# A spectral layer and an MLP on one core: the prologue's loads, splits and fillers rearranged, and the MLP's matmuls issued in a fixed order

## The chip, the core and the metric

The kernel runs on one core of one Trainium2 chip. The core has a matrix engine (TensorE, "PE" in the profile, with its weight loads as "PEld"), three engines for elementwise work (VectorE "DVE", ScalarE "ACT", GpSimd "POOL"), SyncE ("SP"), which here only issues DMAs, and 16 DMA engines shared by all queues. Every engine runs its own instructions in order and waits for others through semaphores. The metric is the device time of one execution in microseconds; lower is better. Three executions of the kernel before took 2612.57, 2615.16 and 2617.0 us, median 2615.16.

## The reference

```python
X = np.fft.rfft(x, axis=1)                      # x: (8, 3008, 256), float32
Yr = Xr @ w_r - Xi @ w_i + b_r                  # w_r, w_i: 256 x 256
Yi = Xr @ w_i + Xi @ w_r + b_i
Yr = np.sign(Yr) * np.maximum(np.abs(Yr) - 0.01, 0.0)   # and the same for Yi
y = np.fft.irfft(Yr + 1j * Yi, n=3008, axis=1)
h = y.reshape(24064, 256) @ w_in                # w_in: 256 x 2048, float64
out = np.maximum(0.01 * h, h) @ w_out           # w_out: 2048 x 256, float64
```

Per batch of 3008 positions: a real Fourier transform along the sequence, a complex 256 x 256 projection with a bias and a soft threshold, the inverse transform; then, over all 24064 tokens, an MLP with a leaky rectifier.

## The kernel before

The transform of 3008 = 47 x 64 points is done in two factors, so it becomes small matrix products. A batch passes three stages. `fwd(b)` is the first: it loads x in seven chunks (six of 512 columns, one of 256), folds the two halves, multiplies by `fa` and writes the result u to DRAM. For batch 1 alone the fold is left out, and `stage_a1(c)` makes chunk c with plain float32 products: eight TensorE matmuls for a wide chunk, two ScalarE copies from PSUM, two SyncE writes. `mid(b)` is the second: 12 steps that load u (`load(j)`, two steps ahead), do the second factor (`stage_b`), the projection, bias and threshold (`proj`), and the inverse's first factor (`stage_g`), whose result v is copied by ScalarE and written to DRAM by two DMAs. `inverse(pi, eh)` is the third: it loads v as `vin`, multiplies by `ga` into a PSUM bank of the tag psf, and with VectorE and ScalarE writes tokens into the tile `yc`.

The MLP (`moe`) works on 47 chunks of 512 tokens. `forms(ci)` makes seven combinations of the four quarters of a chunk (one level of Strassen's scheme) and splits each into a high and a low float32r part, the tiles `yh` and `yl`. A chunk has eight steps q. In a step `moe_a` does four of the seven products and `moe_b` three, each as three float32r matmuls of 256 columns (high by high, low by high, high by low): 12 and 9 matmuls into two PSUM banks of the tag psh. Between them ScalarE copies a product (p), VectorE adds to make u and two more sums in place; `moe_b`'s products accumulate in the same banks, so they wait for these sums. Then VectorE adds (gf), ScalarE applies the rectifier, casts to the high part gh, and VectorE subtracts to make the low part gl. `moe_o(ci, q, eh)` multiplies gh and gl by w_out: six matmuls of 512 columns for each of two halves of the output, two steps (LAG) after the step that made them. The last of a chunk is copied and written to `out`.

What sets the order: the program is written as one sequence, and a planner places each instruction on its engine, by program order and by its own estimate of when inputs and buffers are free. So an engine's queue may hold instructions in another order than the program's. `tc.issue_after(ins)` orders what is issued inside it behind `ins`, on the engine of `ins` only; it is an order in a queue, not a wait on a result. Tiles of one tag share its buffers, and a new tile waits until the oldest holder has been read.

The prologue runs batch 0's `fwd` and `mid` with nothing of the MLP beside them. In it, w_in (stored as float64) is loaded in four parts and converted to float32 pairs (`convert_win`), batch 1's x is loaded, and w_out is loaded by `load_wout`: two reads of 512 KB ordered behind `reads[13]` (a u load) into the buffers of the tag gl, six more into the buffers e and z as these come free. Each of the eight parts of w_out is then converted by three ScalarE and seven VectorE instructions (`float64_parts` and lines 192 to 194); part 0 is converted anywhere in the prologue, the others behind the first chunk's last split (`made`). Five chunks of `stage_a1` follow batch 0's `mid`, behind its last-but-one product (`turning[NPAIR - 2]`); chunks 4 and 5 come at the third and fifth half step of the MLP in program order. `split_consts` splits the projection's weights, `gb` and `fa` into float32r pairs for the other batches, at the ninth half step, behind `made`. Its source `w32` holds a buffer of the tag yl, in which `forms` also places its yl and `stage_a1` its chunk 4. After the first chunk, the other batches' `fwd` and `mid` are spread between the MLP's half steps by a fraction of the work done.

Of the kernel before, what the change touches and what calls it, by code (L numbers as in the profile page):

```python
# [20 lines left out]
P = 128  # L21
# [9 lines left out]
def spectral_mlp_kernel(  # L31
# [48 lines left out]

    def block(dst, l, r, start=False):

        for i, (a, b) in enumerate(((l[0], r[0]), (l[0], r[1]), (l[1], r[0]))):
            nc.tensor.matmul(dst, a, b, start=start and i == 0, stop=i == 2, skip_group_check=True)  # L84
# [47 lines left out]
    made, converted = [], []  # L132
# [34 lines left out]
    def load_wout():  # L167
# [5 lines left out]
        def load(early):  # L173
# [3 lines left out]
            with tc.issue_after(reads[13 if early else -1].ins):  # L177
                sync.dma_start(raw.rearrange("p (a f) w -> p a (f w)", a=n), ov[:, k * n:(k + 1) * n, :])
# [24 lines left out]
    reads, written, turned, turning, thresholded = [], [], [], [], []  # L203
# [6 lines left out]
    def fwd(b):  # L210
# [107 lines left out]
    def mid(b):  # L318
# [4 lines left out]
        pool.memset(zero, 0.0)  # L323
# [94 lines left out]
        def stage_g(j):  # L418
# [6 lines left out]
            for c in range(2):  # L425
                act.dma_start(vd[c, 2 * j:2 * j + 2, :N2, :].rearrange("k n d -> n k d"), v[c * N2:(c + 1) * N2])
# [30 lines left out]
    y_t, v_t, f_t, h_t, g_t, o_t = {}, {}, {}, {}, {}, {}  # L457
# [16 lines left out]
    def inverse(pi, eh):  # L474
# [8 lines left out]
        for c in range(2):  # L483
            for i in range(2):
                o = c * ne + i * n0 * NK1
                nc.tensor.matmul(py[:, o:o + P], vin[:, c, i, s], consts["ga"][:, c, :], start=True, stop=True)  # L486
# [7 lines left out]
        while lo < p0[pi + 1]:  # L494
# [4 lines left out]
            act.copy(f_t[ci][:, eh, lo - ci * NT:hi - ci * NT], y[:, lo - p0[pi]:hi - p0[pi]])  # L499
            lo = hi  # L500

    def forms(ci):
# [7 lines left out]
        def split(k, w):  # L510
            cp = act.copy(yh[:, k], w)  # L511
            return dve.tensor_sub(yl[:, k], w, yh[:, k].bitcast(F32)), cp  # L512
# [12 lines left out]
        if ci == 0:  # L525
            made[:] = last
# [28 lines left out]
    def moe_b(ci, q):  # L555
# [11 lines left out]
        act.copy(gh, g)  # L567
        gl = sb.tile([P, 4, HT], F32R, name="gl", tag="gl")
        dve.tensor_sub(gl, g, gh.bitcast(F32))  # L569
        g_t[ci, q] = (gh, gl)  # L570

    def moe_o(ci, q, eh):
# [6 lines left out]
        for i in range(2):  # L579
            f = 2 * q + i  # L580
            for j, (a, r) in enumerate(((wh, gh), (wl, gh), (wh, gl))):
                nc.tensor.matmul(  # L582
                    po, a[:, f, s], r[:, i], start=(f == 0 and j == 0), stop=(f == NF - 1 and j == 2),
                )
# [28 lines left out]
    def moe():  # L613

        for i, (ci, q) in enumerate(steps):
            if q == 0:
                nxt = tokens(ci + 1) if ci + 1 < nch else iter(())
            moe_a(ci, q)
            if i >= LAG:
                moe_o(*steps[i - LAG], 0)  # L620
            next(nxt, None)
            yield ci + (q + 0.5) / NQ
            if i >= LAG:
                moe_o(*steps[i - LAG], 1)
            moe_b(ci, q)
# [228 lines left out]
```

## Time and profile before

| what | value |
|---|---|
| median of three executions | 2615.16 us |
| the profiled execution | 2613.38 us |
| its span, first to last instruction | 2611.6 us |
| first matmul of the MLP (L84) | 122.1 us |
| last conversion of w_out ends | about 202 us |
| last matmul of `stage_b` (batch 7) starts | 2218.9 us |
| DMA traffic | 165.14 MB, 62 GB/s of HBM over the span |

The profile is of one execution. An engine's row gives busy time, share of the span and the count of instructions. A group's row gives the line of the kernel, engine, operation, the tile written and the tiles read, shapes, the count, then busy time and the mean of one in ns, then the engine's idle time just before them and what ended it. A row of the timeline gives start, length, instruction, and in brackets the idle time ahead of it. SPq and ACTq are DMA issues on SyncE's and ScalarE's queues. A stretch's row is explained where it is shown. Matmuls overlap, so the length of one is more than the distance between two starts.

### The profile page before, as it was taken

What the parts mean: (1) busy time and instruction counts of PE and PEld (TensorE: products, weight loads), DVE (VectorE), ACT (ScalarE), POOL (GpSimd) and SP (SyncE); (2) the same over time, 40 slices, a digit from 0 to 9 for tenths busy, and PEclk for the clock granted to TensorE, in tenths of its full rate; (3) what the DMA queues carried; (4) which work ended last, traced back from release to release, by engine and by line L of the source; (5) the groups of instructions that cost most, each with busy time, mean ns of one, the idle gap of its engine ahead of it and who ended that gap; (6) DMA issues with size and microseconds to landing.
All of it is one profiled execution on the core that took longest, in us unless ns stands there. A gap on an engine that the chain in (4) does not pass through costs nothing. (4 is left out here: it accounts for less than half of the span.)

```text
span 2611.6 us, 42622 instructions
## 1 busy us (share of the span) xinstructions
PE 2555.1 (98%) x16300; PEld 2284.0 (87%) x16300; DVE 1855.0 (71%) x3403; ACT 1655.3 (63%) x3174; POOL 236.7 (9%) x180
## 2 busy tenths in 40 slices
PE   6899999999999999999999999999999999999998
PEld 4578898899889998999989999899998899988887
DVE  5687777776767778677777777777777677665664
ACT  4766675676656666567656666566665666655554
POOL 0000112000210002000121001200012000000000
PEclk8999999999999999999999999999999999999999
DMA  9622113211221113211132211321113211100000
GB/s 267 169 64 59 47 45 109 65 48 51 82 74 52 45 48 86 73 53 54 34 100 63 61 44 37 107 72 48 37 39 112 62 49 41 43 25 24 17 9 17
DMA packets 118437, 165.14 MB, mean 63 GB/s; under 512 B 13437, under 2 KB 69401, under 8 KB 118233
## 3 DMA queue, kind: packets, MB, share of 16 engines
q1 hardware_dynamic: 78193, 116.07, 14.6%
q10 hardware_dynamic: 40040, 46.34, 7.0%
q8 instruction: 128, 2.10, 0.3%
q14 instruction: 76, 0.62, 0.1%
HBM read 86.60 MB, written 75.76 MB: 62 GB/s over the span
## 5 line engine op out<-in xcount | busy, mean ns | idle before, releaser
L84 PE MATMUL psh<-yh,win_hi 128*128 128x256 f32 x2632 | 737.5, 284 | 8.5 <-DVE u L549 4.8
L84 PE MATMUL psh<-yl,win_hi 128*128 128x256 f32 x2632 | 735.3, 281 | 0.8 <-DVE yl L512 0.8
L84 PE MATMUL psh<-yh,win_lo 128*128 128x256 f32 x2632 | 724.8, 280 | 0.0
L582 PE MATMUL pso<-gh,wout_hi 128*128 128x512 f32 x1504 | 598.1, 398 | 7.1 <-ACT gh L567 6.6
L569 DVE TENSOR_TENSOR gl<-gf,gh 128x1024 fp32r<-128x1024 f32 x376 | 466.0, 1240 | 194.0 <-ACT gh L567 192.2
L582 PE MATMUL pso<-gh,wout_lo 128*128 128x512 f32 x1504 | 591.9, 394 | 0.1
L582 PE MATMUL pso<-gl,wout_hi 128*128 128x512 f32 x1504 | 557.3, 396 | 2.7 <-DVE gl L569 1.4
L84 PEld LDWEIGHTS psh<-yh,win_hi 128*128 128x128 f32 x2632 | 493.7, 189 | 34.1 <-DVE u L549 6.2
L84 PEld LDWEIGHTS psh<-yl,win_hi 128*128 128x128 f32 x2632 | 497.6, 189 | 23.7 <-DVE yl L512 1.9
L84 PEld LDWEIGHTS psh<-yh,win_lo 128*128 128x128 f32 x2632 | 493.1, 189 | 3.0
L565 ACT ACTIVATE gf<-gf 128x768 f32<-128x768 f32 x376 | 315.5, 846 | 239.8 <-DVE gf L563 229.8
L563 DVE TENSOR_TENSOR gf<-psh,u 128x512 f32<-128x512 f32 x376 | 258.3, 687 | 236.9 <-PE psh L84 235.2
L567 ACT CAST gh<-gf 128x1024 fp32r<-128x1024 f32 x376 | 394.5, 1050 | 15.6 <-ACT gf L565 9.6
L582 PEld LDWEIGHTS pso<-gl,wout_hi 128*128 128x128 f32 x1504 | 282.7, 188 | 67.7 <-DVE gl L569 12.6
L582 PEld LDWEIGHTS pso<-gh,wout_hi 128*128 128x128 f32 x1504 | 282.9, 188 | 52.4 <-ACT gh L567 11.2
L582 PEld LDWEIGHTS pso<-gh,wout_lo 128*128 128x128 f32 x1504 | 283.1, 188 | 48.9 <-DVE wout_lo L194 0.7
L562 ACT ACTIVATE gf<-psh 128x256 f32<-128x256 f32 x376 | 144.8, 385 | 194.6 <-PE psh L84 174.6
L385 POOL TENSOR_TENSOR kb<-bias,kc 128x512 f32<-128x512 f32 x84 | 118.5, 1410 | 1543.9 <-ACT kc L382 1272.9
L548 ACT COPY p<-psh 128x256 f32<-128x256 f32 x376 | 139.3, 370 | 97.5 <-PE psh L84 91.5
L549 DVE TENSOR_TENSOR u<-psh,p 128x256 f32<-128x256 f32 x376 | 157.2, 418 | 47.8 <-ACT p L548 45.7
L551 DVE TENSOR_TENSOR gf<-psh,u 128x256 f32<-128x256 f32 x376 | 155.8, 418 | 21.0 <-PE psh L84 11.8
L552 DVE TENSOR_TENSOR gf<-psh,gf 128x256 f32<-128x256 f32 x376 | 156.4, 420 | 6.3
(134 smaller groups left out, 3260.8 us busy)
## 6 DMA issues: line engine op xcount, KB each, us to landing
u<-u_dram SPq DMA_DIRECT2D x192, 128.0 KB, 2.7
v_dram<-v ACTq DMA_DIRECT2D x192, 128.0 KB, 2.4
out_dram<-ob SPq DMA_DIRECT2D x94, 256.0 KB, 2.0
vin<-v_dram SPq DMA_DIRECT2D x96, 240.0 KB, 3.3
xin<-x_dram SPq DMA_DIRECT2D x85, 240.0 KB, 2.9
u_dram<-xin ACTq DMA_DIRECT2D x72, 240.0 KB, 2.4
win_raw<-w_in_dram SPq DMA_DIRECT2D x8, 512.0 KB, 6.7
raw<-w_out_dram SPq DMA_DIRECT2D x8, 512.0 KB, 6.5
```

The costliest lines, as they stand in the source:

```text
L84: nc.tensor.matmul(dst, a, b, start=start and i == 0, stop=i == 2, skip_group_check=True)
L385: pool.tensor_add(kb, bias, kc.unsqueeze(1).broadcast_to([P, 2, D]))
L548: act.copy(p1, b1[:, lo])
L549: dve.tensor_add(u2, b1[:, hi], p1)
L551: dve.tensor_add(g[:, 3], b2[:, hi], u2)
L552: dve.tensor_add(g[:, 3], b2[:, lo], g[:, 3])
L562: act.activation(g[:, 0], b1[:, lo], AF.Prelu, alpha=SLOPE)
L563: dve.tensor_add(g[:, 1:3], b2.rearrange("p (k n) -> p k n", k=2), u2.unsqueeze(1).broadcast_to([P, 2, HT]))
L565: act.activation(g[:, 1:4], g[:, 1:4], AF.Prelu, alpha=SLOPE)
L567: act.copy(gh, g)
L569: dve.tensor_sub(gl, g, gh.bitcast(F32))
L582: nc.tensor.matmul(po, a[:, f, s], r[:, i], start=(f == 0 and j == 0), stop=(f == NF - 1 and j == 2),)
```

## The change

Seven edits go together. (1) `split_consts` runs right after batch 0's first stage instead of in the MLP. (2) The v of batch 0 is written to DRAM by SyncE instead of ScalarE. (3) w_out is read by DMAs that GpSimd issues, ordered only behind the first memset of GpSimd in `mid(0)`; the first conversion is ordered behind `made` like the others. (4) Batch 1's first stage is spread: chunks 0 and 1 inside the last steps of `mid(0)`, chunks 2 and 3 behind the last product of `stage_g`, the small chunk 6 behind the first chunk's last inverse, chunks 4 and 5 behind a gh cast and a gl subtraction of the MLP. Their order behind `turning[NPAIR - 2]` goes. (5) Chunks 0 to 3 use the PSUM tag psh, the others psf. (6) Every part of the MLP (a, half of o, b) is ordered on TensorE behind the last matmul of the part before. (7) The program order in a step becomes a, first half of o, b, second half of o; it was a, both halves, b.

```diff
+    mlp = []
+    def in_order(part, *args):
+        with tc.issue_after(mlp[0].ins) if mlp else nullcontext():
+            part(*args)
...
-            nc.tensor.matmul(dst, a, b, start=start and i == 0, stop=i == 2, skip_group_check=True)
+            mlp[:] = [nc.tensor.matmul(dst, a, b, start=start and i == 0, stop=i == 2, skip_group_check=True)]
...
-            with tc.issue_after(reads[13 if early else -1].ins):
-                sync.dma_start(raw.rearrange("p (a f) w -> p a (f w)", a=n), ov[:, k * n:(k + 1) * n, :])
+            with tc.issue_after(zeroed[0].ins):
+                pool.dma_start(raw.rearrange("p (a f) w -> p a (f w)", a=n), ov[:, k * n:(k + 1) * n, :])
...
-            pas = [(bank("psf", 2) if c in (4, 5) else bank("psh", 4))[:PA, :n] for _ in range(2)]
+            pas = [(bank("psh", 4) if c < 4 else bank("psf", 2))[:PA, :n] for _ in range(2)]
             for h in range(2):
-                with tc.issue_after(turning[NPAIR - 2].ins):
-                    products(pas[h], [
-                        (consts[f"fa{h}32"], (x_t[c][0],)), (consts[f"fa{2 * h}32"], (x_t[c][1],))])
+                products(pas[h], [
+                    (consts[f"fa{h}32"], (x_t[c][0],)), (consts[f"fa{2 * h}32"], (x_t[c][1],))])
...
-        pool.memset(zero, 0.0)
+        cleared = pool.memset(zero, 0.0)
+        if b == 0:
+            zeroed.append(cleared)
...
-                act.dma_start(vd[c, 2 * j:2 * j + 2, :N2, :].rearrange("k n d -> n k d"), v[c * N2:(c + 1) * N2])
+                (act if b else sync).dma_start(
+                    vd[c, 2 * j:2 * j + 2, :N2, :].rearrange("k n d -> n k d"), v[c * N2:(c + 1) * N2])
...
+        inverted[:] = [cp, mm]
...
+        cp = act.copy(gh, g)
...
+        parted[:] = [cp, dve.tensor_sub(gl, g, gh.bitcast(F32))]
...
-                nc.tensor.matmul(
+                mlp[:] = [nc.tensor.matmul(
                     po, a[:, f, s], r[:, i], start=(f == 0 and j == 0), stop=(f == NF - 1 and j == 2),
-                )
+                )]
...
-            moe_a(ci, q)
+            in_order(moe_a, ci, q)
             if i >= LAG:
-                moe_o(*steps[i - LAG], 0)
+                in_order(moe_o, *steps[i - LAG], 0)
             next(nxt, None)
             yield ci + (q + 0.5) / NQ
+            in_order(moe_b, ci, q)
             if i >= LAG:
-                moe_o(*steps[i - LAG], 1)
-            moe_b(ci, q)
+                in_order(moe_o, *steps[i - LAG], 1)
...
         act.mul(fa32[:, 2], fa32[:, 1], -1.0)
+        split_consts()
...
         if i == 13:
             next(wout)
+        if i >= 14:
+            if i < 16:
+                next(fp.gen)
...
-    fp.to(0.69)
+    for _ in range(2):
+        with tc.issue_after(turning[-1].ins):
+            next(fp.gen)
...
+    with tc.issue_after(inverted[-1].ins), tc.issue_after(inverted[-2].ins):
+        next(fp.gen)
     for _ in forms(0):
         pass
-    next(wout)
+    with tc.issue_after(made[0].ins):
+        next(wout)
...
         if i in (2, 4):
-            with tc.issue_after(made[0].ins):
+            with tc.issue_after(parted[0].ins), tc.issue_after(parted[1].ins):
                 next(fp.gen)
-        if i == 8:
-            with tc.issue_after(made[0].ins), tc.issue_after(made[1].ins):
-                split_consts()
```

More of the change, by code (lines that the diff above doesn't have):

```diff
@@ L201, in spectral_mlp_kernel @@
     v_dram = {}
-    reads, written, turned, turning, thresholded = [], [], [], [], []
+    reads, written, turned, turning, thresholded, zeroed = [], [], [], [], [], []
     NX = -(-NS // 2)
@@ L485, in inverse @@
                 o = c * ne + i * n0 * NK1
[L486 removed]
+                mm = nc.tensor.matmul(py[:, o:o + P], vin[:, c, i, s], consts["ga"][:, c, :], start=True, stop=True)
         odd = sb.tile([P, 2 * NG * NK1], F32, name="odd", tag="odd", bufs=1)[:, :ne]
@@ L525, in forms @@
         if ci == 0:
-            made[:] = last
+            made[:] = [last]
         yield
```

14 lines of the change are left out of this document (6 added, 8 removed).

## The prediction

> **What bounds the kernel now.** I read the page first, then the table of stretches, then the groups and the timeline of the stretches that lose time.
>
> ```profile
> span 2611.6 us, 42622 instructions
> PE 2555.1 (98%) x16300; PEld 2284.0 (87%) x16300; DVE 1855.0 (71%) x3403; ACT 1655.3 (63%) x3174; POOL 236.7 (9%) x180
> ```
> ```profile
> 139.00:201.40 62.40, 55.14 (x317) 47.53 (x316) 57.70 (x118) 39.89 (x72) 0.00 (x0) 0.92 0.18 53
> 201.40:2281.80 2080.40, 2072.35 (x13593) 1885.80 (x13593) 1521.06 (x2786) 1363.24 (x2641) 235.88 (x174) 1.00 0.21 61
> 2281.80:2597.80 316.00, 311.52 (x1931) 272.81 (x1929) 189.88 (x352) 164.32 (x295) 0.00 (x0) 1.00 0.05 17
> 2597.80:2611.60 13.80, 7.57 (x27) 5.64 (x25) 3.33 (x4) 4.63 (x6) 0.00 (x0) 0.85 0.10 38
> ```
>
> Columns: stretch, length, then busy time (count) of TensorE, its weight loads, VectorE, ScalarE, GpSimd, the granted clock, DMA share, GB/s. TensorE is the bound. No edit changes the number of matmuls, so only its lost time can go. From 201.4 to 2281.8 it idles 2080.4 - 2072.35 = 8 us; the loss sits in the prologue and the tail.
>
> The busy share hides some of it, since overlapping matmuls count as busy. So I take the spacings from the tail's timeline and the counts from its groups.
>
> ```profile
> 2506.60 0.28 PE L84 MATMUL psh<-yh,win_hi 128*128 128x256 f32 x1
> 2510.37 0.28 PE L84 MATMUL psh<-yh,win_lo 128*128 128x256 f32 x1
> ...
> 2515.98 0.40 PE L582 MATMUL pso<-gl,wout_hi 128*128 128x512 f32 x1
> 2517.83 0.28 PE L84 MATMUL psh<-yh,win_hi 128*128 128x256 f32 x1
> ```
> ```profile
> L84 PE MATMUL psh<-yh,win_hi 128*128 128x256 f32 x393 | 110.4, 283 | 0.1
> L582 PE MATMUL pso<-gh,wout_hi 128*128 128x512 f32 x224 | 90.4, 403 | 3.3 <-ACT gh L567 3.3
> ```
>
> The 33 matmuls of 256 columns start within 3.77 us, 0.118 each; eight of 512 within 1.85 us, 0.231 each. A step of the MLP has 21 and 12: 5.25 us. The tail (2281.8 to 2597.8, no spectral work left) holds three such groups of 393 and three of 224; 80 of its 1931 matmuls remain, the inverse's, which have 128 columns and which I set at 0.1 (an estimate, below the 0.118 of 256): 139 + 155 + 8 = 302 us in 316. **The tail loses 14 us**, 0.24 a step, mostly waiting for gh.
>
> The start of the MLP, 139 to 201.4, holds some ten steps:
>
> ```profile
> L84 PE MATMUL psh<-yh,win_hi 128*128 128x256 f32 x74 | 24.1, 326 | 6.4 <-DVE u L549 2.8 <-ACT gf L562 1.6 <-DVE gf L563 1.4
> L194 DVE TENSOR_TENSOR wout_lo<-cva,cvq 128x512 fp32r<-128x512 f32 x7 | 4.8, 681 | 0.0
> L128 DVE TENSOR_SCALAR raw<-cva 128x512 uint32<-128x512 uint32 x7 | 3.0, 422 | 0.1
> ```
>
> Of its 317 matmuls 3x74 at 0.118 and the rest at no more than 0.231 make 26 + 22 = 48 us, less some 2 for short ones, in 62.4: **16 us lost**, while VectorE is busy for 57.7 of 62.4. VectorE bounds this stretch: seven conversions of w_out run in it, each four instructions like L194 and three like L128, 4.0 us.
>
> **The change part by part.**
>
> *Splits early, and the second batch's chunks 4 and 5 after a gh and gl exist.*
>
> ```profile
> 134.16 1.03 DVE L512 TENSOR_TENSOR yl<-yc,yh 128x256 fp32r<-128x256 f32 x2 [6.43 <-ACT xin L286]
> 137.75 0.69 DVE L105 TENSOR_TENSOR wr_lo<-w,wr_hi 128x512 fp32r<-128x512 f32 x1
> 140.10 0.47 DVE L105 TENSOR_TENSOR fa_lo<-fa,fa_hi 120x120 fp32r<-120x120 f32 x2
> ...
> 125.50 8.87 PE L78 MATMUL psf<-xin,fa 120*120 120x512 f32 x16 [1.00 <-DVE y L492]
> 142.18 0.39 PE L84 MATMUL psh<-yh,win_hi 128*128 128x256 f32 x1 [2.77 <-DVE u L549]
> ```
>
> The first chunk's yl needs a buffer of its tag; one holds w32 until the splits are done, the other the second batch's chunk 4. So VectorE idles 6.43 us, and then u stands behind the splits while TensorE waits 2.77 us. Early splits free w32's buffer, and 6.43 us of VectorE's bound stretch start sooner. Against that stands the first conversion of w_out, now tied behind made: +4.0 us, less the splits (L105: three at 0.69, three at 0.28): 2.9 us. Net 6.4 + 2.9 - 4.0 = 5.3 us. Chunks 4 and 5 move 8.87 us of matmuls into a stretch with 16 us free. I take **-5**; ends +2 (conversions stay the limit) and -9 (all of 6.4 and 2.8).
>
> Where the splits go is idle:
>
> ```profile
> 30.88 0.69 DVE L114 TENSOR_TENSOR w<-w_i,w 128x512 f32<-128x512 f32 x1 [7.36 <-DMA w_i<-w_i_dram]
> 32.69 3.75 PE L349 MATMUL psh<-fb,u 128*128 128x128 f32 x16 [11.44 <-DMA u<-u_dram]
> ```
>
> Both engines wait there on loads. Six ScalarE casts and six subtractions of at most 0.69 fit beside the first stage B. I cost them at 0; if the weights landed later, ScalarE's first ef copy would come up to 2.6 us late.
>
> *Spread first stage.* Two chunks go ahead of the end of batch 0's middle.
>
> ```profile
> 90.71 1.13 PE L78 MATMUL psh<-zf,w 128*128 128x512 f32 x2 [1.20 <-ACT zf L406]
> 97.00 1.13 PE L78 MATMUL psh<-zf,w 128*128 128x512 f32 x2 [1.36 <-ACT zf L406]
> 100.75 2.04 PE L78 MATMUL psh<-zf,w 128*128 128x512 f32 x2 [2.63 <-ACT zf L402]
> 113.56 5.31 PE L78 MATMUL psh<-xin,fa 120*120 120x512 f32 x12
> ```
>
> Gaps of 5.2 us take 16 matmuls at 5.31/12 = 0.44, 7.1 us. Their four ScalarE copies wait only where ScalarE waits on the same chain. But this work filled the time from 102.6 until the inverse (first matmul at 111.0):
>
> ```profile
> L486 PE MATMUL psf<-ga,vin x832: 270/275/348, 111.0 to 2486.9; 120*128 120x128 f32 x167
> 123.37 1.13 PE L486 MATMUL psf<-ga,vin 120*128 120x128 f32 x8 [0.87 <-DVE y L492]
> ```
>
> There chunks 2 and 3 (7.1 us) are left for 8.4 us, and the four inverses, which alternate with ScalarE and VectorE, run with nothing beside them until the small chunk: I estimate 4 us of idle against the 2 us of before (0.87, 1.00). Net 5.2 - 1.3 - 2: **-2**; ends -5 and +3.
>
> *Results by SyncE, w_out by GpSimd.*
>
> ```profile
> L426 ACTq DMA_DIRECT2D v_dram<-v x192: 581/600/1750, 54.0 to 2241.8; - x192
> 99.24 0.59 ACT L424 COPY v<-psh 128x512 f32<-128x512 f32 x1 [1.41 <-issue]
> ...
> 20.00:32.00 12.00, 1.25 (x5) 0.55 (x3) 1.80 (x3) 2.81 (x7) 0.00 (x0) 0.65 0.93 290
> 157.08 27.68 SPq L178 DMA_DIRECT2D raw<-w_out_dram x4
> ```
>
> 24 issues of 0.6 us leave ScalarE's queue, but most lie under a running instruction; the visible one cost 1.41. On SyncE each waits for ScalarE's v, and the u loads behind it wait too; these are issued two steps ahead of their use, which covers a v that is late by less than a step. I take -1 (0 to -4, and +1 if that cover fails once). The w_out reads lose their place behind reads[13]: they follow only GpSimd's first memset and the gl buffers, free once the second group of u has been written, about 21 us. Two reads of 512 KB then share DMAs at 290 GB/s that carry batch 0's u to DRAM and back, for which TensorE waits 11.44 us. Wholly ahead they cost 1.05 MB/290 = 3.6 us, wholly behind 0. I take +2, as the queue is 0.93 full. The later reads no longer hold SyncE for 27.68 us; nobody there needs it before the next u loads, so 0. A GpSimd DMA has no row; beside the landing of SyncE's I allow the reads 0 to 2 us more each, with buffers for two conversions.
>
> **Prologue: -5 - 2 - 1 + 2 = -6 us.**
>
> *MLP in fixed order.* Each step becomes a (12 matmuls, 1.42 us), half of o (6 at 0.231: 1.39), b (9, 1.06), other half.
>
> ```profile
> L567 ACT CAST gh<-gf 128x1024 fp32r<-128x1024 f32 x56 | 58.4, 1042 | 0.2
> L565 ACT ACTIVATE gf<-gf 128x768 f32<-128x768 f32 x56 | 44.9, 839 | 58.2 <-DVE gf L563 58.2
> L563 DVE TENSOR_TENSOR gf<-psh,u 128x512 f32<-128x512 f32 x56 | 38.7, 691 | 90.5 <-PE psh L84 90.2
> ...
> 2508.82 0.41 DVE L549 TENSOR_TENSOR u<-psh,p 128x256 f32<-128x256 f32 x1
> 2510.78 1.23 DVE L569 TENSOR_TENSOR gl<-gf,gh 128x1024 fp32r<-128x1024 f32 x1 [1.54 <-ACT gh L567]
> ```
>
> After b come gf 0.69, activation 0.84, gh 1.04, gl 1.23: 3.8 us. Between b and the o that reads them lie o, a, o, b, o, a: 8.1 us. So no o can wait, and the 3.3 us on gh go. b needs p, u and two more sums of u's size after a: p (a quarter of gh's elements, at most 0.4) starts while a's last six matmuls run, so 0.4 + 3x0.41 - 0.7 = 0.9 us, under 1.39. The last step gains too:
>
> ```profile
> 2600.68 0.76 PE L582 MATMUL pso<-gh,wout_hi 128*128 128x512 f32 x1 [2.63 <-ACT gh L567]
> ```
>
> With 18 o matmuls behind the last b (4.2 us) gh comes in time, and the slow clock of that stretch (0.85) goes: -4 (0 to -4.5). Of the tail's 14 I take -10 (0 to -14), of the middle's 8 idle us -4 (0 to -8), since there the inverse and the spectral work still interrupt. **MLP: -18.**
>
> Sum -24. The profiled execution took 2613.38 us, 1.8 beside its span, and lies 1.8 under the median 2615.16: 2591.
>
> **The rivals.**
>
> 1. *Slower: b waits for VectorE.* The fixed order takes 1.39 us from the slack ahead of b, and behind a waiting b all of TensorE's queue stands: the other half of o, the next a, the spectral matmuls. If gl of step i is served ahead of u of step i+1, the sums are ready 3.8 + 3x0.41 = 5.05 us after b; o, a, o last only 4.20: 0.85 us a step. Before it was 5.59. It decides where VectorE picks gl first. Price: 0.85 in each of 56 tail steps, 48. The middle has 2080/310 = 6.7 us a step, some 0.7 of other matmuls in that path, so 0.15 x 310 = 46. With the prologue's -6, without the -18: 2703 everywhere; on half of the steps 2656; on a quarter, 2633, which I take. Against it: in the tail of before VectorE served u at 2508.82 and idled 1.54 us before gl.
>
> 2. *The prologue gives back its gain.* The early w_out reads cost all of 3.6 and an idle stretch brings half clock, as here:
>
> ```profile
> 139.00:143.50 4.50, 1.26 (x8) 0.85 (x7) 4.50 (x15) 2.98 (x10) 0.00 (x0) 0.96 0.24 85
> 143.50:153.40 9.90, 8.91 (x39) 8.33 (x40) 9.90 (x22) 6.70 (x12) 0.00 (x0) 0.50 0.01 2
> ```
>
> 9.9 us at clock 0.50 cost 5. After the change such idle could fall at the inverse. Then the prologue is about +3: 2615 + 3 - 18 = 2600. By the Trainium skill ("TensorE: Matmul & The Clock Gate", "What's actually happening") an idle window of about 3.4 us halves the clock until a busy one has passed; these rows agree, with 1.26 us of work in 4.5.
>
> 3. *The order changes nothing in the tail or middle* (the stall only moves to b): prologue and end, 2615 - 6 - 4 = 2605.
>
> 4. *GpSimd's reads come late.* Six reads stand amid the conversions, where VectorE is full. If each waited for the three L128-like instructions of a conversion, 3 x 0.42 x 6 = 8 us on a VectorE-bound stretch: 2599. The Trainium skill ("SBUF — State Buffer", "Who interferes with whom") says that descriptors made by GpSimd are blocked while VectorE runs a tensor_scalar in its two-port mode; no run here shows it.
>
> 5. *The edits cancel, or the fillers do not land in the gaps:* 2615.
>
> **How the numbers follow.** Forecast 0.44, rival 1 0.18, rival 2 0.12, rival 3 0.10, rival 4 0.06, rival 5 0.10. A measurement of this kernel tells 0.2% (5 us) from no change. Faster: 0.44 + 0.12 + 0.10 + 0.06 = 0.72; same 0.10; slower 0.18. The forecast's own range adds the ends of its terms part way, 2574 to 2607. Rival 5 and the near end of rival 1 take the upper end to 2626; below, 2572 leaves out little.
>
> **What would show it.** L105 before 40 us; no 6.43 wait of L512; TensorE's gaps of 1.36 and 2.63 filled with xin,fa; the L349 wait at 32.7 starting at most 4 us later; 201.4's last conversion some 5 us earlier; the tail at 42 to 43 us per eight steps instead of 45, with runs of 12, 6, 9, 6. Wrong if L84 waits on L552 in most tail steps, or if L349 starts beyond 37 us.

## The result, and the profile after

| kernel | median us | ratio to before, 95% interval |
|---|---|---|
| before, beside the changed kernel | 2616.08 | |
| the changed kernel | 2890.16 (2888.82 to 2892.13) | 1.105 [1.1031, 1.1069] |

The change makes the kernel 274 us slower. The forecast (2591, range 2572 to 2626) is wrong, in sign and in size. Its first rival named the mechanism and priced it far too low.

First come lines of the page after: the span, the busy times, the chain by engine, and two of the groups.

```profile
span 2890.3 us, 43048 instructions
...
PE 2673.7 (93%) x16300; PEld 2307.6 (80%) x16300; DVE 1892.0 (65%) x3403; ACT 1671.0 (58%) x3174; POOL 248.9 (9%) x188
...
PE 46%; DVE 27%; ACT 18%; issue 4%; DMA 3%; POOL 1%; SPq 0%; DVEq 0%; ACTq 0%; POOLq 0%
...
L92 PE MATMUL psh<-yh,win_hi 128*128 128x256 f32 x2632 | 791.7, 301 | 113.9 <-DVE gf L563 78.3
...
L580 DVE TENSOR_TENSOR gl<-gf,gh 128x1024 fp32r<-128x1024 f32 x376 | 465.2, 1237 | 441.6 <-ACT gh L578 434.2
```

The number of matmuls is the same 16300, but TensorE is busy for 93% in place of 98%, and the chain that ended last, which before could be followed over 20% of the span alone (17% TensorE, 3% other engines), now goes through VectorE (27%) and ScalarE (18%). L92 is the block matmul of a and b (L84 before). It waited 113.9 us in all, mostly for the last of the three sums (L563). `gl` (L580) in its turn waited 434 us for the cast gh, almost always: VectorE takes it the moment that the cast is done.

One step of the tail shows the chain. The rows are from the timeline of the changed kernel, TensorE first, then VectorE and ScalarE.

```profile
2612.18 0.28 PE L92 MATMUL psh<-yh,win_lo 128*128 128x256 f32 x1
...
2615.09 0.40 PE L593 MATMUL pso<-gh,wout_hi 128*128 128x512 f32 x1
...
2616.24 0.39 PE L593 MATMUL pso<-gl,wout_hi 128*128 128x512 f32 x1
2616.80 0.38 PE L92 MATMUL psh<-yh,win_hi 128*128 128x256 f32 x1 [0.17 <-DVE u L560]
...
2617.79 0.39 PE L92 MATMUL psh<-yh,win_hi 128*128 128x256 f32 x1 [0.37 <-DVE gf L563]
...
2612.50 0.69 DVE L574 TENSOR_TENSOR gf<-psh,u 128x512 f32<-128x512 f32 x1 [1.07 <-PE psh L92]
2615.19 1.22 DVE L580 TENSOR_TENSOR gl<-gf,gh 128x1024 fp32r<-128x1024 f32 x1 [1.99 <-ACT gh L578]
2616.33 0.42 DVE L560 TENSOR_TENSOR u<-psh,p 128x256 f32<-128x256 f32 x1
2616.85 0.42 DVE L562 TENSOR_TENSOR gf<-psh,u 128x256 f32<-128x256 f32 x1
2617.31 0.42 DVE L563 TENSOR_TENSOR gf<-psh,gf 128x256 f32<-128x256 f32 x1
...
2613.23 0.85 ACT L576 ACTIVATE gf<-gf 128x768 f32<-128x768 f32 x1 [1.69 <-DVE gf L574]
2614.11 1.05 ACT L578 CAST gh<-gf 128x1024 fp32r<-128x1024 f32 x1
2615.06 0.36 ACT L559 COPY p<-psh 128x256 f32<-128x256 f32 x1
```

The last matmul of b starts at 2612.18. From there it goes gf (2612.50), activation (2613.23), gh (2614.11); p of the next step stands behind gh on ScalarE (2615.06), gl ahead of u on VectorE (2615.19, 2616.33); the sums end at 2617.73. TensorE has half an o, a and half an o to do meanwhile, and its last o row starts at 2616.24. The next row but for the waits would start 0.23 later, at 2616.47; it starts at 2616.80, 0.33 late. Between 2616.80 and 2617.79 stand three matmuls of 0.118, 0.35; the rest, 0.64, is a second wait. So **about 1 us is lost in this step**, where by the forecast's count a step of the tail lost 0.24 before. The profile's waits show only part of it (here 0.17 and 0.37 us), since the row of the matmul ahead reaches into the gap. The waits by stretch, first steps 16 to 304 of the changed kernel, then its tail from step 304 on (us in all, times, longest):

```profile
PE psh L92 <- DVE gf L563: 45.9, 91, 2.0
PE psh L92 <- DVE u L560: 20.4, 61, 1.1
PE psf L78 <- ACT eh L373: 16.2, 9, 2.8
PE psf L78 <- DVE xz L266: 11.6, 24, 1.8
```
```profile
PE psh L92 <- DVE gf L563: 26.3, 63, 1.7
PE psh L92 <- DVE u L560: 10.2, 54, 0.5
```

In the tail the wait for the last sum is there in 63 of 71 steps. In the middle it is listed 91 times in 288 steps, and the spectral matmuls (L78) wait there too. Counted from VectorE's rows, u comes right behind a gl in 62 of the last 72 steps and in 155 of the 288 before them.

Where the time went, by the start of ScalarE's copy p of a step (L559 after, L548 before; 376 steps), for all kernels that are told of below. Each row is of one execution, and the executions of one kernel lie up to 9 us apart:

```
us between                    p of step 0   0 to 16  16 to 304  304 to 375  375 to end of span
before                              139.1     103.8     1943.3       403.8      21.6
changed kernel                      136.7     127.2     2145.1       466.8      14.5
fixed order + program a,o,b,o       141.8     124.3     2145.2       465.6      14.1
prologue alone                      136.6     105.2     1943.5       403.9      21.9
prologue + fixed, a,o,o,b           136.8     116.0     1948.3       393.9      15.1
prologue + a,o,b,o, not fixed       136.0     103.6     1945.7       404.8      20.7
changed, gl late                    135.7     126.6     2001.7       416.8      13.7
changed, gl and gh late             134.5     112.8     1971.7       398.7      13.9
prologue, fixed from step 304       135.4     105.1     1942.4       396.5      15.1
prologue, w_out by SyncE            127.7     103.0     1944.3       403.6      20.4
same, fixed from step 304           129.5     103.4     1942.2       395.8      14.7
only later w_out reads by GpSimd    134.0     105.5     1942.0       403.7      20.6
w_out by SyncE, not spread          129.9     103.1     1942.5       404.3      20.4
w_out by SyncE, v by ScalarE        131.4     103.0     1944.5       403.8      21.3
```

Against the kernel with the prologue's edits alone, the changed one loses 202 us between steps 16 and 304 (0.70 a step), 63 in the last 71 steps (0.89), 22 in the first 16, and wins 7 at the end.

### The profile page after: what moved, and what is told of

It is laid out like the page before. It is cut to its first block, busy times and chain, and to the rows that moved or that the text cites. A ratio compares the mean times of both kernels' runs of the same rounds, so it can differ in the third digit from the quotient of the medians.

```text
span 2890.3 us, 43048 instructions
## 1 busy us (share of the span) xinstructions
PE 2673.7 (93%) x16300; PEld 2307.6 (80%) x16300; DVE 1892.0 (65%) x3403; ACT 1671.0 (58%) x3174; POOL 248.9 (9%) x188
## 4 chain that ended last, share of the span: by engine, by line
PE 46%; DVE 27%; ACT 18%; issue 4%; DMA 3%; POOL 1%; SPq 0%; DVEq 0%; ACTq 0%; POOLq 0%
PE psh L92 18%; PE pso L593 16%; PE psf L78 7%; DVE gl L580 7%; ACT gh L578 6%; ACT gf L576 5%; DVE gf L574 4%; DVE gf L562 3%; DVE u L560 2%; DVE gf L563 2%; PE psf L496 2%; PE psf L358 2%; ACT zf L415 2%; DVE yl L523 1%; ACT zf L411 1%
## 5 line engine op out<-in xcount | busy, mean ns | idle before, releaser
L92 PE MATMUL psh<-yh,win_hi 128*128 128x256 f32 x2632 | 791.7, 301 | 113.9 <-DVE gf L563 78.3
L580 DVE TENSOR_TENSOR gl<-gf,gh 128x1024 fp32r<-128x1024 f32 x376 | 465.2, 1237 | 441.6 <-ACT gh L578 434.2
L92 PE MATMUL psh<-yl,win_hi 128*128 128x256 f32 x2632 | 741.1, 282 | 0.0
L92 PE MATMUL psh<-yh,win_lo 128*128 128x256 f32 x2632 | 739.4, 281 | 0.0
L92 PEld LDWEIGHTS psh<-yh,win_hi 128*128 128x128 f32 x2632 | 499.5, 190 | 235.1 <-DVE gf L563 122.9
L593 PE MATMUL pso<-gl,wout_hi 128*128 128x512 f32 x1504 | 594.5, 395 | 0.0
L92 PEld LDWEIGHTS psh<-yl,win_hi 128*128 128x128 f32 x2632 | 500.4, 190 | 23.6 <-issue 0.6
L92 PEld LDWEIGHTS psh<-yh,win_lo 128*128 128x128 f32 x2632 | 499.3, 190 | 0.3 <-issue 0.2
L394 POOL TENSOR_TENSOR kb<-bias,kc 128x512 f32<-128x512 f32 x84 | 127.1, 1513 | 1616.0 <-ACT kc L391 1507.9
L563 DVE TENSOR_TENSOR gf<-psh,gf 128x256 f32<-128x256 f32 x376 | 157.8, 420 | 6.1
L559 ACT COPY p<-psh 128x256 f32<-128x256 f32 x376 | 137.2, 365 | 14.9 <-PE psh L92 13.0
```

What stands on the lines that cost most here:

```text
L92: mlp[:] = [nc.tensor.matmul(dst, a, b, start=start and i == 0, stop=i == 2, skip_group_check=True)]
L559: act.copy(p1, b1[:, lo])
L563: dve.tensor_add(g[:, 3], b2[:, lo], g[:, 3])
L580: parted[:] = [cp, dve.tensor_sub(gl, g, gh.bitcast(F32))]
L593: mlp[:] = [nc.tensor.matmul(po, a[:, f, s], r[:, i], start=(f == 0 and j == 0), stop=(f == NF - 1 and j == 2),)]
```

## The experiments

They are numbered in the order in which they were set up and told in the order of the argument. "Kernel 2" is the kernel of experiment 2.

**1. The order alone.** The kernel before, with edits (6) and (7) and none of the prologue's.

```diff
...
+    def in_order(part, *args):
+
+        with tc.issue_after(mlp[0].ins) if mlp else nullcontext():
+            part(*args)
...
+            in_order(moe_b, ci, q)
             if i >= LAG:
-                moe_o(*steps[i - LAG], 1)
-            moe_b(ci, q)
+                in_order(moe_o, *steps[i - LAG], 1)
...
```

> The kernel before with the fixed order and the new program order in a step (a, half of o, b, half of o), and no edit of the prologue. Order theory (O): in the tail after the change VectorE served the 1.22 us gl of a step ahead of the next step's u, and b waited 1.1 us in each step; that alone makes nearly the whole loss of 274 us. It expects 2860 to 2900 us here, 6.2 to 6.3 us per step in the tail. Prologue theory (P), by which the prologue's edits leave queues in a worse order for the whole run, expects under 2700 us. A theory that any fixed order is slow (F), since nothing can fill a wait, expects the same as O here.

Measured: 2893.69 us, 1.1059 [1.1044, 1.1074]. The order alone makes the whole loss, at 52.2 us per eight steps of the tail, as in the changed kernel. That refutes theory P; O and F are told apart by experiment 3.

**2. The prologue alone.** The changed kernel with free placement and the old program order.

```diff
-        with tc.issue_after(mlp[0].ins) if mlp else nullcontext():
+        with nullcontext():
...
-            in_order(moe_b, ci, q)
             if i >= LAG:
                 in_order(moe_o, *steps[i - LAG], 1)
+            in_order(moe_b, ci, q)
```

> The changed kernel without the fixed order and with the old program order in a step (a, both halves of o, b): the prologue's edits alone. O and F expect 2600 to 2625 us: the prologue's terms as forecast sum to -6 us, but the changed kernel's trace shows stage B 5.7 us later and step 8 at 196.0 instead of 182.4, most of which O puts down to the order. P expects over 2800 us.

Measured: 2609.64 us, 0.9973 [0.9963, 0.9983]: 7 us faster than before, close to the -6 of the forecast's sum for the prologue. Its terms, though, are not those of the forecast (experiments 7, 10, 11, 12).

**3. Fixed order with the old program order.** As 2, but the fixed order stays: a, o, o, b.

```diff
-            in_order(moe_b, ci, q)
             if i >= LAG:
                 in_order(moe_o, *steps[i - LAG], 1)
+            in_order(moe_b, ci, q)
```

> The changed kernel with its fixed order, but the old program order in a step: a, both halves of o, b. Between b and the next b then lie a and both halves of o, 4.2 us, and all 2.78 us of o after a. O expects the wait gone, since the sums come 5.05 us after b and the path is 1.39 us longer than after the change, 5.59: 5.25 to 5.4 us per step in the tail and 2575 to 2610 us in all. F expects 2750 us or more, as the order is as fixed as before.

Measured: 2610.8 us, 0.9975 [0.9966, 0.9985], 0.8 above the range of O, with 5.41 us per step in the tail (43.3 per eight). The wait is gone, so a fixed order as such is not what costs, and theory F falls.

**5. The new program order, not fixed.** The changed kernel with free placement.

```diff
-        with tc.issue_after(mlp[0].ins) if mlp else nullcontext():
+        with nullcontext():
```

> The changed kernel without the fixed order, but with the program order a, o, b, o; the planner is free to place the matmuls. Theory S (the planner takes program order as a rank, so the program order alone puts b ahead of the second o): TensorE shows 12, 6, 9, 6 as in the changed kernel, b waits for VectorE in most steps, 2860 to 2900 us. Theory F (the planner moves b behind what is ready, so only the two together lose): 2600 to 2640 us, L92 waits on L563 for under 20 us in all.

Measured: 2612.71 us, 0.9981 [0.9971, 0.9991]. So of the four combinations three lie within 4 us of each other, and the fourth is 280 us slower: neither the fixed order nor the program order costs much by itself. Here L92 waits on L563 for 0.6 us in all. The timelines of the tail show the pattern that repeats there (matmuls of the MLP in a row, a for those of a and b; the first three patterns cover two steps, the others one):

```
before                 o16 a9 o8 a33
2, prologue alone      o16 a9 o8 a33
5, a,o,b,o not fixed   o16 a9 o8 a33
changed kernel         a12 o6 a9 o6
3, a,o,o,b fixed       a21 o12
```

Left free, TensorE runs the same pattern whatever the program order; fixed in the new order, half an o is all that b's sums have to hide behind. VectorE and ScalarE in the tail of kernel 3, from its timeline:

```profile
2390.34 0.69 DVE L574 TENSOR_TENSOR gf<-psh,u 128x512 f32<-128x512 f32 x1 [1.07 <-PE psh L92]
2391.44 0.42 DVE L560 TENSOR_TENSOR u<-psh,p 128x256 f32<-128x256 f32 x1 [0.41 <-ACT p L559]
2391.97 0.42 DVE L562 TENSOR_TENSOR gf<-psh,u 128x256 f32<-128x256 f32 x1
2392.42 0.42 DVE L563 TENSOR_TENSOR gf<-psh,gf 128x256 f32<-128x256 f32 x1
2393.26 1.23 DVE L580 TENSOR_TENSOR gl<-gf,gh 128x1024 fp32r<-128x1024 f32 x1 [0.42 <-ACT gh L578]
...
2391.03 0.37 ACT L559 COPY p<-psh 128x256 f32<-128x256 f32 x1 [1.02 <-PE psh L92]
2391.30 0.85 ACT L576 ACTIVATE gf<-gf 128x768 f32<-128x768 f32 x1
2392.18 1.05 ACT L578 CAST gh<-gf 128x1024 fp32r<-128x1024 f32 x1
```

With b directly ahead of a, p comes on ScalarE before the activation and the cast (2391.03), and u and the sums before gl: nobody has to choose (u right behind a gl in none of the last 72 steps). The half o moved from before b to behind it lets the activation and the cast run first, and they are what p and u then stand behind.

**4. gl late.** The changed kernel, with each gl ordered on VectorE behind the next step's sums.

```diff
-        dve.tensor_add(g[:, 3], b2[:, lo], g[:, 3])
+        last = dve.tensor_add(g[:, 3], b2[:, lo], g[:, 3])
+        while late:
+            gl, gp, gh = late.pop(0)
+            with tc.issue_after(last.ins):
+                parted[1:] = [dve.tensor_sub(gl, gp, gh.bitcast(F32))]
...
-        parted[:] = [cp, dve.tensor_sub(gl, g, gh.bitcast(F32))]
+        parted[:1] = [cp]
+        if ci == nch - 1 and q == NQ - 1:
+            dve.tensor_sub(gl, g, gh.bitcast(F32))
+        else:
+            late.append((gl, g, gh))
...
```

> The changed kernel with its fixed order and its new program order, but each gl subtraction is ordered on VectorE behind the next step's three sums. Nothing else moves. O expects the wait of b to go: p still stands behind the gh cast on ScalarE, so up to 0.2 us per step may stay; 5.25 to 5.5 us per step in the tail, 2575 to 2640 us in all. F expects 2750 us or more.

Measured: 2695.78 us, 1.0297 [1.0283, 1.0311]. Moving this one VectorE instruction takes back 194 of the 274 us, but not all: the time misses the ranges of both theories, and the tail takes 5.71 us per step where O expected at most 5.5. O had allowed only 0.2 us per step for p behind gh. The timeline shows what was left, on VectorE and ScalarE:

```profile
2455.04 0.42 DVE L560 TENSOR_TENSOR u<-psh,p 128x256 f32<-128x256 f32 x1 [2.26 <-ACT p L559]
...
2453.69 1.05 ACT L582 CAST gh<-gf 128x1024 fp32r<-128x1024 f32 x1
2454.64 0.36 ACT L559 COPY p<-psh 128x256 f32<-128x256 f32 x1
```

VectorE is free, and idles 2.26 us for p, which stands right behind the cast on ScalarE, as in 57 of the last 72 steps.

**8. gl and gh late.** As 4, with the cast ordered behind the next step's p as well.

```diff
-        act.copy(p1, b1[:, lo])
+        first = act.copy(p1, b1[:, lo])
+        casts = []
+        while late:
+            gl, gp, gh = late.pop(0)
+            with tc.issue_after(first.ins):
+                casts.append((gl, gp, gh, act.copy(gh, gp)))
...
-        cp = act.copy(gh, g)
...
```

> The changed kernel with both the gh cast of a step behind the next step's p on ScalarE and its gl subtraction behind the next step's sums on VectorE. Theory O (in the changed order b waits because gh and gl work of the last step stands ahead of p, u and the sums): both causes are gone, eight tail steps take 42 to 43.5 us and L92 waits on L563 for under 15 us in all; 2575 to 2625 us. Rival (VectorE and ScalarE have no more room in a step, so the late gl delays gf of the next step, and so on): the wait moves to gf or to gh, eight tail steps stay at 45 to 46 us, 2680 to 2700 us.

Measured: 2635.96 us, 1.0074 [1.0058, 1.0089]. The tail is close to what theory O asked for: 43.8 us per eight steps against 42 to 43.5 (262.9 us from p of step 320, at 2318.2, to p of step 368, at 2581.1), and far from the rival's 45 to 46. The whole missed its 2575 to 2625, since 26 us more than in kernel 2 remain. The profiled executions lie 20.5 us apart: 8 more in the first 16 steps and 28 from 16 to 304, less 2 before step 0, 5 in the tail and 8 at the end. Its waits of b for the sums between steps 16 and 304:

```profile
PE psh L92 <- DVE gf L568: 10.2, 22, 1.1
PE psh L92 <- DVE u L565: 5.0, 8, 1.7
```

15 of the 28 us are listed here, against 66 in the changed kernel. Why these steps and not others was not tried.

**6. Fixed only in the tail.** All prologue edits, program order a, o, o, b, and the fixed order from step 304 on; the diff is against the changed kernel.

```diff
-        with tc.issue_after(mlp[0].ins) if mlp else nullcontext():
+        ci, q = args[:2]
+        late = ci * NQ + q >= 304 - (LAG if len(args) == 3 else 0)
+        with tc.issue_after(mlp[0].ins) if mlp and late else nullcontext():
...
-            in_order(moe_b, ci, q)
             if i >= LAG:
                 in_order(moe_o, *steps[i - LAG], 1)
+            in_order(moe_b, ci, q)
```

> All prologue edits, program order a, o, o, b, and the fixed order only from step 304 of 376 on. Theory T (a fixed order costs where spectral work and conversions have to fit in, and pays where only the MLP is left): the steps up to 304 as in the kernel with the prologue edits alone, the last 56 steps at 43.5 us per eight in place of 45.3, and a short end: 11 us less in the tail and 6 less behind it, 2588 to 2596 us. Rival: the tail's gain in the kernel fixed throughout was time that it had lost before (work left over was less or more), so little is left of it: 2604 to 2611 us.

Measured: 2596.26 us, 0.9919 [0.9907, 0.9932]. Theory T holds, at the upper end of its range: 7.4 us less in the last 71 steps than with the prologue alone (403.9 to 396.5; it expected 11), 6.8 less behind them (21.9 to 15.1). Fixed throughout (kernel 3), the gains of 10.0 and 6.8 there were eaten by 10.8 us in the first 16 steps and 4.8 from 16 to 304.

**7. w_out by SyncE.** The prologue alone, but w_out read as before the change.

```diff
-            with tc.issue_after(zeroed[0].ins):
-                pool.dma_start(raw.rearrange("p (a f) w -> p a (f w)", a=n), ov[:, k * n:(k + 1) * n, :])
+            with tc.issue_after(reads[13 if early else -1].ins):
+                sync.dma_start(raw.rearrange("p (a f) w -> p a (f w)", a=n), ov[:, k * n:(k + 1) * n, :])
```

> The prologue edits alone (no fixed order, program order a, o, o, b), but w_out is read by SyncE again, the first two reads behind the fourteenth u load. Theory W (the early reads take DMA time from u's way to DRAM and back): the first stage B starts 4 to 6 us earlier than 38.4, near 33, and the middle of batch 0 ends that much earlier; if it reaches the end, 2604 to 2607 us. Rival (the prologue's loss is made up by VectorE, which is the limit again at the conversions, or the late reads then come late): stage B starts earlier, and the time stays at 2608 to 2613 us.

Measured: 2602.11 us, 0.9944 [0.9931, 0.9956]: 7.5 us better than kernel 2, more than theory W gave. The diff is against kernel 2. The next rows are from the timelines of kernel 2 (TensorE, ScalarE, GpSimd) and then of kernel 7 (TensorE, ScalarE).

```profile
37.60 2.69 PE L358 MATMUL psh<-fb,u 128*128 128x128 f32 x11 [14.58 <-DMA u<-u_dram]
...
34.70 0.62 ACT L112 CAST wr_hi<-w 128x512 fp32r<-128x512 f32 x1 [9.42 <-DMA w<-w_r_dram]
...
22.38 0.85 POOL L186 DMA_DIRECT2D raw<-w_out_dram  x1 [21.32 <-DMA u_dram<-xin]
23.50 0.73 POOL L186 DMA_DIRECT2D raw<-w_out_dram  x1 [0.28 <-ACT xin L276]
```
```profile
31.98 3.75 PE L358 MATMUL psh<-fb,u 128*128 128x128 f32 x16 [9.75 <-DMA u<-u_dram]
...
28.88 0.62 ACT L112 CAST wr_hi<-w 128x512 fp32r<-128x512 f32 x1 [4.39 <-DMA w<-w_r_dram]
```

With two reads of 512 KB free to start at 22 us, the projection's weights come 5.8 us later and stage B 5.6. (Stage B starts at 33.47 in kernel 10, which has the early reads of kernel 7, so some 1.5 of the 5.6 may be scatter.)

**10. Only the six later reads by GpSimd.** Again against kernel 2.

```diff
-            with tc.issue_after(zeroed[0].ins):
-                pool.dma_start(raw.rearrange("p (a f) w -> p a (f w)", a=n), ov[:, k * n:(k + 1) * n, :])
+            with tc.issue_after((reads[13] if early else zeroed[0]).ins):
+                (sync if early else pool).dma_start(raw.rearrange("p (a f) w -> p a (f w)", a=n), ov[:, k * n:(k + 1) * n, :])
```

> Prologue edits alone, the first two w_out reads by SyncE behind the fourteenth u load, the six later ones by GpSimd. Theory W (what costs is that 1.05 MB stand ahead of u and the projection's weights at 22 to 34 us): stage B starts near 32 and the time is that of the kernel with all reads by SyncE, 2600 to 2604 us. Rival G (GpSimd's later reads come late beside VectorE's conversions): conversions late by several us, 2606 to 2611 us.

Measured: 2607.68 us, 0.9966 [0.9953, 0.9979]. Theory W falls short: the later reads cost as well, 5.8 us against kernel 7 (0.9966 less 0.9944, of 2616), which leaves 1.7 for the early ones, not told from zero, though stage B came 4 to 5.6 us later with them: how much of that is caught up stays open. The time lies in the range of rival G, but the loss is there before its conversions: p of step 0 comes at 134.0 in kernel 10 and at 127.7 in kernel 7, and from there to step 304 both take 2047 us. (The conversions do take longer, 62.9 us from the first `wout_lo` to the last against 60.2, and that is made up by step 304.) The timeline of ScalarE at the end of batch 0's middle shows what comes late, with GpSimd's first late read, kernel 10 first, then kernel 7.

```profile
100.56 0.85 POOL L186 DMA_DIRECT2D raw<-w_out_dram  x1 [5.67 <-PE psf L78]
...
102.71 0.82 ACT L411 COPY zf<-t 64x256 f32<-64x256 f32 x2
107.40 0.68 ACT L131 ACTIVATE cvq<-raw 128x512 f32<-128x512 uint32 x1 [3.87 <-DMA raw<-w_out_dram]
109.22 0.59 ACT L433 COPY v<-psh 128x512 f32<-128x512 f32 x1 [1.15 <-DMA v_dram<-v]
```
```profile
101.88 0.82 ACT L411 COPY zf<-t 64x256 f32<-64x256 f32 x2
104.13 0.59 ACT L433 COPY v<-psh 128x512 f32<-128x512 f32 x1 [1.44 <-PE psh L78]
```

`cvq<-raw` begins the third conversion of w_out. Its read starts as soon as its buffer is free (100.56), and the instruction stands on ScalarE ahead of batch 0's last v; there it waits 3.87 us for the read, and v, its write and the inverse's `vin` behind it come 5.1 us later than in kernel 7 (109.22 less 104.13), of which 0.8 stood before (102.71 less 101.88). With SyncE's read the same instruction comes behind that v, at 117.97. The changed kernel has the wait too:

```profile
108.03 0.70 ACT L131 ACTIVATE cvq<-raw 128x512 f32<-128x512 uint32 x1 [2.53 <-DMA raw<-w_out_dram]
```

**11. First stage not spread.** Kernel 7 with chunks 0 to 3 behind the last-but-one product of `stage_g` again.

```diff
-        if i >= 14:
-            if i < 16:
-                next(fp.gen)
...
-    for _ in range(2):
-        with tc.issue_after(turning[-1].ins):
+    for _ in range(4):
+        with tc.issue_after(turning[NPAIR - 2].ins):
             next(fp.gen)
```

> As the kernel with prologue edits and SyncE's w_out reads, but chunks 0 to 3 of the second batch's first stage all stand behind the last-but-one product of stage_g again (chunk 6, 4 and 5 stay where the change has them). If spreading them fills TensorE's gaps at the end of the middle, this one is later by 2 to 5 us (2604 to 2607 us); if the inverse's chain, idle beside it, takes the gain back, 2600 to 2603 us.

Measured: 2600.28 us, 0.9936 [0.9923, 0.9949]: no later than kernel 7, within the intervals. Spreading these chunks gains nothing that can be told.

**12. v by ScalarE.** Kernel 7, with batch 0's v written by ScalarE again.

```diff
-                (act if b else sync).dma_start(
+                act.dma_start(
```

> As the kernel with prologue edits and SyncE's w_out reads, but batch 0's v is written by ScalarE again. If the 24 issues of 0.6 us on ScalarE's queue stand in the chain of the middle of batch 0, its end is 1 to 4 us later and the time 2603 to 2606 us; if they lie under running instructions, 2600 to 2603 us.

Measured: 2603.82 us, 0.995 [0.9937, 0.9963]. The step is 1.7 us in the medians, in the expected direction and inside the intervals, so it is not told from zero.

**9. The two that paid, together.** Kernel 6 with the edit of kernel 7.

```diff
-            with tc.issue_after(zeroed[0].ins):
-                pool.dma_start(raw.rearrange("p (a f) w -> p a (f w)", a=n), ov[:, k * n:(k + 1) * n, :])
+            with tc.issue_after(reads[13 if early else -1].ins):
+                sync.dma_start(raw.rearrange("p (a f) w -> p a (f w)", a=n), ov[:, k * n:(k + 1) * n, :])
```

> Two of the changes that paid, together: w_out read by SyncE as before the change, and the fixed order with program order a, o, o, b from step 304 on; the other prologue edits stay. If the two gains are independent (one lies before 128 us, the other behind 2180 us): 2596.3 less 7.5, so 2587 to 2591 us. If the earlier prologue is eaten in the middle, where the spectral stages set the pace: 2592 to 2597 us.

Measured: 2587.16 us, 0.9885 [0.987, 0.9901], **the fastest of all, 30 us under before**, and at the sum of the two gains. Its stretch from step 304 to 375 in the table of stretches (columns as in the prediction):

```profile
2175.10:2570.90 395.80, 395.01 (x2545) 357.57 (x2544) 270.52 (x472) 230.69 (x412) 4.60 (x3) 1.00 0.08 24
```

TensorE is idle for 0.8 us of 395.8 there (busy counts overlapping matmuls).

## Why the prediction was wrong, point by point

- **The bound.** Right: TensorE bounds, and what can be had lies in the prologue and the tail. Kernel 9 takes its 30 us from these two and about 1 us from the middle.
- **"So b's sums need 0.4 + 3x0.41 - 0.7 = 0.9 us, under 1.39." This is the step that failed.** It took VectorE and ScalarE to be free when a ends. By the rows of the step above, counted from the start of the o behind a (2615.09), p starts 0.03 us before it and not 0.7, since gh stands ahead of p on ScalarE; u starts 1.24 us behind it (2616.33), since gl stands ahead of u on VectorE; and the sums end 2.64 us behind it (2617.73), not 0.9. The two stand there because the forecast's own credit, "no o can wait" for gh, came with moving activation, gh and gl into exactly the stretch in which p, u and the sums are due. Experiments 4 and 8 show each part: gl alone 194 us, gl and gh 254 of the 274. What is left of it, 20 us, was not traced to a cause.
- **Rival 1** had the mechanism, the place and the path: sums ready 5.05 us after b against 4.20 of matmuls, 0.85 a step. Measured from b's last start it is 5.55 (2617.73 less 2612.18), and the tail paid 0.89 a step against kernel 2. Two sizes were wrong. It was taken on a quarter of the steps, where VectorE picks gl first; the tail shows the wait in 63 of 71 (u right behind a gl in 62 of 72), because the choice is hardly open: p is copied behind the cast that makes gl ready. And for the middle it allowed 0.15 a step, as 0.7 of other matmuls would fill the wait; measured 0.70. That the spectral stages bring VectorE and ScalarE work as well as matmuls may be why; it was not tried. With 0.89 and 0.70 its own sum, 2615 - 6 + 0.89 x 56 + 0.70 x 310, gives 2876 in place of "2703 everywhere".
- **The evidence against rival 1** was one row of the old order, and the row behind it says the opposite. VectorE served u at 2508.82 and then idled ahead of gl (2510.78); the next u comes right behind that gl:

```profile
2511.92 0.42 DVE L549 TENSOR_TENSOR u<-psh,p 128x256 f32<-128x256 f32 x1
```

  In the last 72 steps of before u comes right behind a gl 32 times. Before, 16 o in a row stood on TensorE to cover it (the pattern above); after, six.
- **MLP: tail -10, end -4, middle -4.** The first two came in their sum where the order was a, o, o, b and fixed in the tail alone, which is not the order of the change: 14.1 us (0.9973 less 0.9919, of 2616), 7.4 in the last steps and 6.8 behind. That the tail's 14 were "mostly waiting for gh" rests on 3.3 us that its row lists; the rest was not attributed. The middle went the other way: fixing it costs 4.8 us there and 10.8 at the start. There VectorE also serves conversions and spectral work, and a fixed order leaves no choice of what runs meanwhile; that this is the reason is argued from the stretch in which it happens, not shown by itself.
- **Prologue -6.** Measured -7, from terms that partly cancel. *w_out by GpSimd, +2 (0 to 3.6)*: 7.5 us, mis-sized. The bound 3.6 counted the bytes of the two early reads and nothing else. With them stage B alone came 4 to 5.6 us later (the path writes u and reads it back, and the weights share it). By experiment 10 more of the cost lies with the later reads, through the wait on ScalarE's queue that ends at 107 us, which the forecast did not count. The trace of before has such waits for these reads too, 2.57 us at 119.05 and 0.88 at 120.60, but behind the last v. *Spread first stage, -2*: nothing to be told, by experiment 11. *v by SyncE, -1*: 1.7, not told from zero. *Splits early and chunks 4, 5 later, -5 (ends +2, -9)*: not run alone; kernel 7 has these with the spread, v and the PSUM tags of edit (5), and is 14.7 us under before, so by the difference some 13 are left for them, beyond the end at -9. That is argued, not shown. The p of step 0 comes 11.4 us earlier in kernel 7 (127.7 against 139.1), and the forecast counted the wait of 6.43 and the 2.77 but gave no credit for the 8.87 us of chunks 4 and 5, which stood on TensorE between the first matmul of the MLP (122.1) and that p.
- **Rival 4, GpSimd's reads late beside VectorE**: the cost came (experiment 10), but not by this mechanism. The issues of 140 to 200 us, first kernel 7, then kernel 10 with its stretch:

```profile
raw<-w_out_dram SPq DMA_DIRECT2D x4, 512.0 KB, 3.7
```
```profile
raw<-w_out_dram POOLq DMA_DIRECT2D x4, 512.0 KB, 4.2
```
```profile
140.00:200.00 60.00, 53.35 (x315) 43.89 (x314) 54.79 (x106) 39.78 (x72) 2.90 (x4) 1.00 0.25 73
```

  VectorE is busy for 54.79 of these 60 us (the third busy time). GpSimd's four reads land 4.2 to 4.9 us after their issue. For SyncE's only one landing is on record (3.7), and ScalarE's waits for the other three end 3.6 to 4.5 us after their issue. The lockout that the Trainium skill describes ("SBUF — State Buffer", "Who interferes with whom") would hold a read for whole VectorE instructions; little more than 1 us per read can be of this kind here, and none of it is left by step 304.
- **What would show it.** As listed: the splits came before 40 us and TensorE ran 12, 6, 9, 6; but stage B started beyond 37 us (38.4), which the list gave as a sign of failure; eight tail steps took 52.2 us and not 42 to 43; L92 waited for the last sum in 63 of the tail's 71 steps. The listed signs were the right ones.

## What to carry to other kernels

Before a queue is fixed, write down for each engine what becomes ready between the producer and the consumer in the new order, and who is ahead of whom there: moving half an o changed no dependence, but put three long instructions of the last step ahead of two short ones on which TensorE waited, in nearly every step of the tail and in about half of the others. In this kernel a fixed order paid where one repeating stage was left alone, and cost where other stages had to be fitted in, so it was worth fixing by stretch. Two loads that were free to start early brought a round trip through DRAM 4 to 5.6 us late, and an instruction that consumed a third stood ahead of the critical one on its engine's queue and waited there: look for both before a load is set free.

## What was not expected of the hardware

The waits of the changed kernel slowed TensorE's clock now and then. One case in its tail: the row in which TensorE waits, then the stretch around it and the one behind it (the granted clock is the third number from the end).

```profile
2426.65 0.39 PE L78 MATMUL psf<-wr_hi,eh 128*128 128x256 f32 x1 [2.04 <-DVE yc L529]
```
```profile
2424.00:2427.50 3.50, 1.46 (x9) 1.17 (x9) 3.42 (x9) 3.05 (x8) 0.00 (x0) 1.00 0.00 0
2427.50:2431.50 4.00, 4.00 (x16) 3.42 (x15) 2.65 (x6) 1.95 (x3) 0.00 (x0) 0.57 0.28 66
```

After 2.04 us of waiting the clock is at 0.50 for some 3.4 us (3.4 at 0.50 and 0.6 at 1.00 make the 0.57). Between steps 16 and 375 the changed kernel has 15 such stretches, after waits of 1.0 to 2.8 us; kernel 2 has one. Not every such wait brings one: behind a wait of 2.04 us that ends at 281.2 the clock stays at 1.00. Over the whole tail little of it shows:

```profile
2409.00:2875.80 466.80, 425.91 (x2489) 354.52 (x2488) 259.66 (x457) 222.61 (x390) 1.29 (x1) 0.99 0.06 19
```

TensorE is idle for 41 of 467 us there, and the clock is 0.99 in the mean. In the prologue TensorE stands still from 23.6 to 38.4 us, and the clock falls to 0.50 at 28 us:

```profile
28.00:32.00 4.00, 0.00 (x0) 0.00 (x0) 0.00 (x0) 0.00 (x0) 0.00 (x0) 0.50 0.96 310
```

The Trainium skill ("TensorE: Matmul & The Clock Gate", "What's actually happening") gives an idle window of about 3.4 us for the halving. The prologue agrees; in the tail less than that was enough, and the measurement decides. At 1.7 us each, the 15 stretches are worth at most some 25 of the 274 us, so nearly all of the loss is waiting and not a slower clock.
